# One product of the output stage computed by Strassen's method once more, with a sign flip, sums added by DMA, and work moved between VectorE, ScalarE and GpSimd

## The chip, the cores and the metric

The kernel runs on one core of a Trainium2 chip. The metric is the device time of one execution, in microseconds. The kernel before takes 2399.43 us, the median of three runs that lie between 2399.35 and 2399.5.

Five engines work beside each other and wait for each other through semaphores: TensorE (PE; its weight loads are shown apart as PEld), VectorE (DVE), ScalarE (ACT), GpSimd (POOL) and SyncE (SP, which here only starts DMAs). Each has one stream of instructions in a fixed order.

## The reference

The reference is a short causal convolution along the sequence, followed by a two-layer feed-forward block with a hard-swish gate. All is fp32.

```python
# x (8, 4096, 192), weight (8, 7), moe_w_in (192, 2048), moe_w_out (2048, 192)
w = softmax(weight, axis=-1)                       # per head, 7 taps
out = np.einsum('hk,bskhg->bshg', w, x_unf)        # x_unf: 7 shifted copies of x
h = out.reshape(B * S, D) @ w_in                   # 32768 tokens, 192 -> 2048
relu6 = np.clip(h + 3.0, 0.0, 6.0)
g = h * relu6 / 6.0
return (g @ w_out).astype(np.float32)              # 2048 -> 192
```

## The kernel before

**Tiling.** The 32768 tokens are cut into 32 blocks of 1024. A block has two groups of 512 tokens: group 0 lies on partitions 0 to 63 of the tile `x` and of its convolved form `y`, group 1 on partitions 64 to 127; a DMA (`swap`) copies the halves crosswise, so that each half of the partitions has its own group and the other one (`OWN`, `OTHER`). Block 0 has a path of its own. Blocks 1 to 31 go through two stages, one block after the other, and nearly all of the time is in them.

**The h stage** (`h_phase`, about 38 us a block) computes h = y @ w_in and the gate. It goes by 4 units of the hidden dimension, each with a lower (L) and an upper (U) stream of matmuls on the two halves of TensorE's rows. The order within a unit is written out by hand in `FIRST`, `SECOND` and `OTHERS`: `LP7` is "lower stream, product P7", `LAF` is the VectorE addition at L415 that makes one psum bank out of another one and a saved one, `R` is the relu on ScalarE (L329), `G` the gate on VectorE (L333). A prime means that the step belongs to the unit before, so the last gates of unit u are in the plan of unit u+1. `LP7` accumulates into the bank that `LAF` has just read, so it has to wait for `LAF`; it is the sixth product of the lower stream. `X` stands for what the block before left over (a transpose and its stores).

The result is `g`, in four blocks: `A11` and `A21` are the first half of the hidden dimension for groups 0 and 1, `A12` and `A22` the second half.

**The output stage** (`out_strassen`, about 36 us a block, for blocks 1 to 30; `out_last` for block 31) computes g @ w_out as a 2 by 2 block product in Strassen's form (Winograd's variant): seven products A11·B11, A12·B21, S4·B22, A22·T4, S1·T1, S2·T2, S3·T3, where the S are sums of blocks of g and the T sums of blocks of `w_out`. Each has 96 output rows, as three pieces of 32; TensorE runs four pieces side by side on four column groups. `a11_round` is one round of such matmuls: it computes two of the three pieces of A11·B11 by Strassen's method once more (matmuls 256 tokens wide at L545) and fills the round with the third piece, a piece of A12·B21 and a half of another. Then come `three(4, 2, 1)` (A22·T4), `rest_of_2` (L598), and three rounds for S3, S2 and S4, each with a third of S1·T1 as its fourth stream.

**Who makes the sums.** S3 (L517, 128x1024 for each unit) and the four sums for the inner Strassen of A11 (`a11_sums`, L537, 128x256) are on GpSimd, unit by unit in the h stage; those of the last unit run when the output stage has begun. S1 = A21 + A22 is added in place by DMA (L443). S2 and S4 are on VectorE (L517, two instructions of 128x2048 each).

**VectorE's order in the output stage** is that of the program: the last gates of the h stage; the seven taps of the next block's convolution (L271 and L275, 128x1536 each); seven small additions of the round just computed (L641, 32x256); S2; three additions and one more small one for A12·B21; S4; the output sums, transposes and stores, among them `y_sums` (L296) for the next block; and then `LAF` of the next block's h stage.

Of the kernel before, what the change touches and what calls it, by code (L numbers as in the profile page):

```python
# [16 lines left out]
def kernel(  # L17
# [7 lines left out]
):  # L25

# [24 lines left out]
    G = 2  # L51
# [102 lines left out]
    w_q = cst.tile([P, 4, UNITS, QS], F32, name="w_q")  # L154
# [64 lines left out]
    def w_sums():  # L219

        def sub(out, x, y):
            nc.gpsimd.tensor_tensor(out=out, in0=x, in1=y, op=ALU.subtract)

        for o, x, y in ((T1, B12, B11), (T3, B22, B12), (T2, B22, T1), (T4, T2, B21)):
            sub(w_out[:, :, o], w_out[:, :, x], w_out[:, :, y])
        y11, y12, y21, y22 = (
            w_out[:, c::2, B11, q * QS : (q + 1) * QS] for c in range(2) for q in range(2)
        )
        t1, t2, t3, t4 = (w_q[:, j] for j in range(4))
        for o, x, y in ((t1, y12, y11), (t3, y22, y12), (t2, y22, t1), (t4, y21, t2)):  # L230
            sub(o, x, y)
        b11, b12, b21, b22 = (w_in[:, c::2, s] for s in range(2) for c in range(2))
        t1, t2, t3, t4 = (w_in_t[:, j] for j in range(4))
        for o, x, y in ((t1, b12, b11), (t3, b22, b12), (t2, b22, t1), (t4, b21, t2)):
            sub(o, x, y)
# [24 lines left out]

    def conv_units(i, parts, cuts=1):


        x = x_tiles.pop(i)
        W = N // cuts

        def tap(part, k, t):
            c = c_sb[:, k : k + 1]
            to = y[:, part, t : t + W]
            if k == 0:  # L270
                nc.vector.tensor_scalar(  # L271
                    out=to, in0=x[:, part, t : t + W], scalar1=c, scalar2=None, op0=ALU.mult
                )
            else:
                nc.vector.scalar_tensor_tensor(  # L275
                    out=to, in0=x[:, part, k + t : k + t + W], scalar=c, in1=to,
                    op0=ALU.mult, op1=ALU.add,
                )

        return [  # L280
            lambda part=part, k=k, t=t: tap(part, k, t)
            for part in parts for k in range(KC) for t in range(0, N, W)
        ]
# [44 lines left out]
    def relu(r6, h):  # L328
        nc.scalar.activation(r6, h, ACT.Relu, bias=half[:], scale=1.0 / 6.0)  # L329
# [48 lines left out]
    class Unit:  # L378
# [7 lines left out]
        def run(self, op):  # L386
# [13 lines left out]
            if op in mms:  # L400
                to, w, third = mms[op]
                first = op in ("P1", "P5")
                if first:
                    bank[to] = take()
                half_mm(k, bank[to], w, third, first, True, not first)
            elif op == "F1":
                bank["b"] = take()
                nc.scalar.copy(out=psum[:, bank["b"]], in_=psum[:, bank["a"]])  # L408
            elif op == "CE":
                self.p5 = p5s.tile([P, N], F32, name="p5")  # L410
                nc.scalar.copy(out=self.p5[:], in_=psum[:, bank["e"]])  # L411
                give(bank["e"])
            elif op in ("AF", "AD"):
                to = bank[op[1].lower()] = take()
                nc.vector.tensor_tensor(  # L415
                    out=psum[:, to], in0=psum[:, bank["b"]], in1=self.p5[:], op=ALU.add
                )
            elif op[0] == "R":
                r6 = self.r6[op[1]] = rs.tile([P, N], F32, name="r6")
                relu(r6[:], psum[:, bank[op[1]]])  # L420
            else:
                group, c = self.results[op[1]]
                b = bank[op[1]]
                gate(g_of(2 * u + c, group, k), self.r6[op[1]][:], psum[:, b])
                give(b)

    def h_phase(left):
        work = {(u, k): Unit(u, k) for u in range(UNITS) for k in range(2)}
        for u, plan in enumerate(PLANS):
            for step in plan:  # L430
                if step == "X":
                    while left:
                        left.pop(0)()
                    continue
                op = step[1:].rstrip("'+")
                at = u + (step[-1] == "+") - (step[-1] == "'")
                if at < UNITS:
                    work[at, "LU".index(step[0])].run(op)
            if u:
                slots = slice(2 * u - 2, 2 * u)  # L440
                g_sums(nc.gpsimd, (3,), range(NP)[slots], 2)

                nc.gpsimd.dma_start(  # L443
                    out=S1[:, slots], in_=A22[:, slots], accum_op=ALU.add
                )
            if u < UNITS:
                a11_sums(u)
# [32 lines left out]
    def out_direct(i, work):  # L480

        parts = [(k, q) for k in range(G) for q in range(G * NQ)]
        for r in range(0, len(parts), 4):
# [17 lines left out]
            xt = ot.tile([P, N], F32, name="xt")  # L501
            nc.vector.transpose(out=xt[:], in_=bank)
# [4 lines left out]
    def g_sums(engine, which, slots, width):  # L507

        forms = {
            3: (S3, A11, A21, ALU.subtract),  # L510
            2: (S2, S1, A11, ALU.subtract), 4: (S4, A12, S2, ALU.subtract),
        }
        for n in which:
            o, a, b, op = forms[n]
            for p in slots[::width]:
                r = slice(p, p + width)
                engine.tensor_tensor(out=o[:, r], in0=a[:, r], in1=b[:, r], op=op)  # L517

# [9 lines left out]
    X11, X12, X21, X22 = (A11[:, c::2, t : t + TH] for t in (0, TH) for c in range(2))  # L528

    def a11_sums(u):  # L530

        s1, s2, s3, s4 = (sums[:, n, u] for n in range(4))
        for o, a, b, op in (
            (s1, X21[:, u], X22[:, u], ALU.add), (s3, X11[:, u], X21[:, u], ALU.subtract),
            (s2, s1, X11[:, u], ALU.subtract), (s4, X12[:, u], s2, ALU.subtract),
        ):
            nc.gpsimd.tensor_tensor(out=o, in0=a, in1=b, op=op)  # L537
# [15 lines left out]
    def a11_round(i, p1, p2):  # L553

        ba, bb = take(), take()
        a, b = (psum[:, n] for n in (ba, bb))
        y11, y12, y21, y22 = (
            w_out[:, k::2, B11, q * QS : (q + 1) * QS] for k in range(2) for q in range(2)
        )
        t1, t2, t3, t4 = (w_q[:, n] for n in range(4))  # L560
        s1, s2, s3, s4 = (sums[:, n] for n in range(4))
        m0 = (
            quarters(a, 0, first_half, X11, y11) + quarters(a, 0, second_half, X12, y21)
# [3 lines left out]
            quarters(a, 1, first_half, X22, t4)  # L567
            + quarters(a, 1, second_half, A12[:, ::2, first_half], w_out[:, ::2, B21, rows(2)])
            + quarters(b, 1, first_half, s1, t1) + quarters(b, 1, second_half, s4, y22)
        )  # L570
        m2, m3 = product(a, 2, 1, 2), product(a, 3, 2, 0)
        for n in range(NP):
            for mms, k in ((m0, 2 * n), (m1, 2 * n), (m2, n), (m3, n),
                           (m0, 2 * n + 1), (m1, 2 * n + 1)):
                mms[k]()
        mp = cs.tile([P, TH], F32, name="mp")
        r1, r2, r3 = (mp[rows(n)] for n in range(3))
        nc.scalar.copy(out=r1, in_=a[rows(0), first_half])
        piece(p1, 2, a, 2)
        piece(p2, 0, a, 3)  # L580
        add(p1[rows(0), first_half], r1, a[rows(0), second_half])
        add(r2, r1, b[rows(0), first_half])
        add(r3, r2, b[rows(0), second_half])
        add(p1[rows(0), second_half], r3, a[rows(1), first_half])
        add(p1[rows(1), second_half], r3, b[rows(1), first_half])
        add(r2, r2, b[rows(1), first_half])
        add(p1[rows(1), first_half], r2, b[rows(1), second_half])
# [3 lines left out]
    def rest_of_2(a):  # L591
# [3 lines left out]
        w = w_out[:, :, B21, rows(2)]  # L595
        for p, tokens in ((1, slice(0, N)), (0, second_half)):
            for j in range(4):
                nc.tensor.matmul(  # L598
                    out=bank[rows(j), tokens], lhsT=w[:, 2 * j + p],
                    rhs=A12[:, 2 * j + p, tokens], start=bool(p), stop=True,  # L600
                    tile_position=(0, j * QS), skip_group_check=True,
                )
# [40 lines left out]
    def store(i, c, k, half_, qs=range(NQ), queues=(nc.sync,), tokens=slice(0, N)):  # L643

        xt = ot.tile([P, N], F32, name="xt")
# [4 lines left out]

    def sums_tiles():
        return (cs.tile([DH, N], F32, name=f"c{k}") for k in range(6))
# [3 lines left out]
    def out_last(i):  # L656
# [19 lines left out]
        add(u2[:], p1[:], bank[m])  # L676
# [4 lines left out]
        add(p4[two], u3[two], p4[two], ALU.subtract)  # L681
# [7 lines left out]
        for t in range(0, N, N // 2):  # L689
# [9 lines left out]
            add(u3[rows(2), ts], u3[rows(2), ts], bank[rows(NQ), ts], ALU.subtract)  # L699
# [3 lines left out]
    def out_strassen(i, conv):  # L703
# [3 lines left out]
        ba, a = a11_round(i, p1, p2)  # L707
        g_sums(nc.vector, (2,), every, 4)
        b, bank = three(4, 2, 1)
        nc.scalar.copy(out=p4[:], in_=bank[m])  # L710
        piece(p2, 1, bank, NQ)
        give(b)
        swap(slice(0, K3))
        b, bank = rest_of_2(a)
        pieces(p2, 2, bank)
        give(b)
        add(p2[rows(2), first_half], p2[rows(2), first_half], a[rows(1), second_half])
        give(ba)
        g_sums(nc.vector, (4,), every, 4)
# [7 lines left out]
        add(u2[:], p1[:], bank[m])  # L727
# [3 lines left out]
        add(p4[:], u3[:], p4[:], ALU.subtract)  # L731
# [27 lines left out]
    with tc.manual_schedule():  # L759
# [115 lines left out]
        cs = ctx.enter_context(tc.tile_pool(name="cs", bufs=1))  # L875
        ot = ctx.enter_context(tc.tile_pool(name="ot", bufs=4))
# [8 lines left out]
        sums = ss.tile([P, 4, UNITS, N // 2], F32, name="sums")  # L885
        left = []
        for i in range(1, NB):
            h_phase(left)
# [39 lines left out]
```

## Time and profile before

The page of the profile has a span of 2397.1 us.

| engine | busy us | share |
|---|---|---|
| PE | 2388.7 | 100% |
| DVE | 2138.0 | 89% |
| PEld | 1105.0 | 46% |
| ACT | 1087.9 | 45% |
| POOL | 836.4 | 35% |

One block (block 10) in stretches, from the profile's table of busy time by window. It starts with the h stage at 764.28 us and ends where the next h stage starts.

| stage | us | PE | DVE | ACT | POOL |
|---|---|---|---|---|---|
| h stage | 38.08 | 38.08 | 31.79 | 27.79 | 20.01 |
| `a11_round` | 6.90 | 6.90 | 6.80 | 1.26 | 5.61 |
| `three(4, 2, 1)` | 6.87 | 6.87 | 6.73 | 1.52 | 0.00 |
| `rest_of_2` | 1.29 | 1.29 | 1.29 | 1.00 | 0.00 |
| S3, S2, S4 rounds | 20.72 | 20.72 | 20.19 | 1.90 | 0.00 |
| sum | 73.86 | 73.86 | 66.79 | 33.47 | 25.62 |

A matmul counts as busy from its start to its modelled end, and the next has started by then, so PE reads as busy throughout even where a start is late. DVE is busy nearly all of the output stage and has its idle time in the h stage.

### The profile page before, as it was taken

The page shows a single profiled execution, that of the slowest core. Times are in us where ns is not written, and L with a number is a line of the kernel's source. Part 1 is how long each engine was busy: PE and PEld are TensorE (multiplying, and loading weights), DVE is VectorE, ACT ScalarE, POOL GpSimd, SP SyncE. Part 2 cuts the span into 40 slices and gives each one's busy share as a digit, 9 for nine tenths or more (in the row PEclk, how much of TensorE's full clock was granted, in tenths as well). Part 3 has the DMA queues.
Part 4 walks back from the last instruction along what each step waited for, and adds up shares of the span by engine and source line. Part 5 has one row for each costly group of instructions (what it writes and reads, how often), then busy time and mean ns, then how long its engine had stood idle before and what let it go on. Part 6 is the DMA issues. An engine that isn't in the chain of part 4 may idle for free.

```text
span 2397.1 us, 43036 instructions
## 1 busy us (share of the span) xinstructions
PE 2388.7 (100%) x17496; PEld 1105.0 (46%) x17496; DVE 2138.0 (89%) x2773; ACT 1087.9 (45%) x1858; POOL 836.4 (35%) x780
## 2 busy tenths in 40 slices
PE   9999999999999999999999999999999999999998
PEld 6444444444444444444454444444444444444443
DVE  8798889988899988899888998889998889988896
ACT  7234553345543355433454334553445543455433
POOL 2524432234422344223443224432234422344222
PEclk9999999999999999999999999999999999999999
DMA  5233333323333233333333333333323233333322
GB/s 146 46 56 64 62 61 64 67 50 69 59 59 66 53 73 60 60 58 57 67 63 58 67 57 59 63 67 58 67 52 73 54 65 59 55 70 63 58 51 43
DMA packets 261143, 149.86 MB, mean 63 GB/s; under 512 B 207504, under 2 KB 212624, under 8 KB 260944
## 3 DMA queue, kind: packets, MB, share of 16 engines
q1 hardware_dynamic: 225880, 81.56, 16.9%
q0 software_dynamic: 33824, 65.28, 15.8%
q8 instruction: 137, 2.24, 0.4%
q14 instruction: 62, 0.51, 0.1%
q10 hardware_dynamic: 1240, 0.27, 0.1%
HBM read 31.72 MB, written 25.17 MB: 24 GB/s over the span
## 4 chain that ended last, share of the span: by engine, by line
PE 99%; DMA 0%; DVE 0%; SPq 0%; ACT 0%; issue 0%; DVEq 0%; ACTq 0%
PE psum L323 51%; PE psum L456 41%; PE psum L545 5%; PE psum L598 2%; DMA x<-in_x_dram 0%; DMA out_dram<-xt 0%; DVE c L641 0%; DVE xt L647 0%; SPq L106 0%; SPq L140 0%; DVE top L184 0%; PE psum L774 0%; DVE y L275 0%; SPq L95 0%; ACT y L788 0%
## 5 line engine op out<-in xcount | busy, mean ns | idle before, releaser
L456 PE MATMUL psum<-g,w_out 128*32 128x512 f32 (+1 forms) x7936 | 1120.0, 589 | 0.0
L323 PE MATMUL psum<-y,w_in 64*128 64x512 f32 x3664 | 884.8, 591 | 0.4 <-DVE y L275 0.3
L329 ACT ACTIVATE r<-psum,half 128x512 f32<-128x512 f32 x1024 | 641.0, 688 | 241.6 <-PE psum L323 234.8
L333 DVE SCALAR_TENSOR_TENSOR g<-r,psum 128x512 f32<-128x512 f32 x1024 | 641.7, 681 | 4.7 <-ACT r L329 1.5
L323 PEld LDWEIGHTS psum<-y,w_in 64*128 64x128 f32 x3664 | 441.6, 187 | 362.6 <-issue 292.2
L537 POOL TENSOR_TENSOR sums<-g 128x256 f32<-128x256 f32 x248 | 188.1, 831 | 1181.3 <-DVE g L333 1163.2
L456 PEld LDWEIGHTS psum<-g,w_out 128*32 128x32 f32 x7936 | 339.4, 110 | 460.3 <-issue 438.1
L323 PE MATMUL psum<-y,w_in_t 64*128 64x512 f32 x1984 | 524.5, 593 | 0.0
L415 DVE TENSOR_TENSOR psum<-psum,p 128x512 f32<-128x512 f32 x496 | 324.5, 694 | 193.1 <-PE psum L323 184.7
L633 ACT COPY c<-psum 32x512 f32<-32x512 f32 x218 | 126.0, 578 | 588.2 <-PE psum L456 571.0
L517 POOL TENSOR_TENSOR s<-g 128x1024 f32<-128x1024 f32 x124 | 293.8, 2369 | 245.5 <-PE psum L323 237.7
L275 DVE SCALAR_TENSOR_TENSOR y<-x,c_sb,y 128x1536 f32<-128x1536 f32 (+1 forms) x206 | 366.5, 1786 | 6.6
L323 PEld LDWEIGHTS psum<-y,w_in_t 64*128 64x128 f32 x1984 | 247.7, 186 | 195.2 <-issue 124.9
L517 DVE TENSOR_TENSOR g<-g 128x2048 f32<-128x2048 f32 x124 | 279.5, 2296 | 7.4 <-DMA g<-g 3.9
L456 PE MATMUL psum<-s,w_out 128*32 128x512 f32 x1488 | 218.9, 592 | 0.0
L408 ACT COPY psum<-psum 128x512 f32<-128x512 f32 x248 | 138.8, 571 | 71.7 <-PE psum L323 56.1
L443 POOL DMA_DIRECT2D g<-g x124 | 149.1, 1202 | 39.8 <-POOL s L517 39.8
L641 DVE TENSOR_TENSOR c<-c,psum 32x512 f32<-32x512 f32 (+2 forms) x219 | 139.8, 638 | 16.0 <-ACT c L633 9.7
L411 ACT COPY p<-psum 128x512 f32<-128x512 f32 x248 | 133.2, 591 | 41.1 <-PE psum L323 40.3
L456 PEld LDWEIGHTS psum<-s,w_out 128*32 128x32 f32 x1488 | 70.8, 110 | 129.2 <-issue 124.8
L545 PE MATMUL psum<-g,w_out 128*32 128x256 f32 x720 | 109.4, 380 | 0.0
L545 PE MATMUL psum<-sums,w_q 128*32 128x256 f32 x720 | 108.5, 379 | 0.0
(64 smaller groups left out, 1080.1 us busy)
## 6 DMA issues: line engine op xcount, KB each, us to landing
g<-g POOLq DMA_DIRECT2D x124, 512.0 KB, 5.0
out_dram<-xt SPq DMA_DIRECT2D x380, 64.0 KB, 2.0
y<-y SPq DMA_DIRECT2D x62, 384.0 KB, 4.7
x<-in_x_dram SPq DMA_DIRECT2D x55, 388.5 KB, 6.0
stage<-in_moe_w_in_dram SPq DMA_DIRECT2D x16, 192.0 KB, 4.4
stage<-in_moe_w_out_dram SPq DMA_DIRECT2D x8, 384.0 KB, 5.1
x<-in_x_dram SPq DMA_DIRECT2D x7, 384.0 KB
y<-y SPq DMA_DIRECT2D x6, 128.0 KB, 2.4
```

The costliest lines, as they stand in the source:

```text
L275: nc.vector.scalar_tensor_tensor(out=to, in0=x[:, part, k + t : k + t + W], scalar=c, in1=to, op0=ALU.mult, op1=ALU.add,)
L323: nc.tensor.matmul(out=psum[:, b], lhsT=w[r], rhs=y[r, third_of_y], start=start, stop=stop, skip_group_check=onto,)
L329: nc.scalar.activation(r6, h, ACT.Relu, bias=half[:], scale=1.0 / 6.0)
L333: nc.vector.scalar_tensor_tensor(out=out, in0=r6, scalar=1.0, in1=h, op0=ALU.min, op1=ALU.mult)
L408: nc.scalar.copy(out=psum[:, bank["b"]], in_=psum[:, bank["a"]])
L415: nc.vector.tensor_tensor(out=psum[:, to], in0=psum[:, bank["b"]], in1=self.p5[:], op=ALU.add)
L443: nc.gpsimd.dma_start(out=S1[:, slots], in_=A22[:, slots], accum_op=ALU.add)
L456: lambda p=p: nc.tensor.matmul(out=bank[j * QS : (j + 1) * QS, tokens], lhsT=w_out[:, p, w, cols], rhs=x[:, p, tokens], start=(first and p ...
L517: engine.tensor_tensor(out=o[:, r], in0=a[:, r], in1=b[:, r], op=op)
L537: nc.gpsimd.tensor_tensor(out=o, in0=a, in1=b, op=op)
L545: lambda u=u: nc.tensor.matmul(out=dst[rows(j), tokens], lhsT=w[:, u], rhs=x[:, u], start=(u == 0 and tokens == first_half), stop=(u == UN ...
L641: nc.vector.tensor_tensor(out=out, in0=x, in1=y, op=op)
```

## The change

The change does the following for blocks 1 to 30.

- A22·T4 gets the same treatment as A11·B11: `round_twice(1, ...)` replaces `three(4, 2, 1)`. Its inner sums (`quarter_sums(engine, 1, u)`, four of 128x256 for each unit) are added; `rest_of_2` shrinks, since the second round takes another half piece of A12·B21 with it. TensorE has fewer matmuls for it.
- Group 1 is negated: the taps use `c_sg`, whose upper half is minus the coefficients, the relu is given scale -1/6 for group 1, and so A21 and A22 come out with a minus sign. S2 is now a plain sum, S1 + A11, and a DMA with accumulation can make it: three quarters of it (slots 2 to 7) are added by three DMAs from GpSimd's queue, one quarter stays on VectorE.
- The first tap of the convolution goes from VectorE to ScalarE.
- The sums of the last unit (S3 of it, and the inner sums of A22) go to VectorE; the other units' stay on GpSimd.
- Work tiles of the output stage and the transposed tiles share memory with the inner sums.

```diff
-            if k == 0:
+            if k == 0 and i:
+                nc.scalar.mul(to, x[:, part, t : t + W], c)
...
+            last = u == UNITS
             if u:
+                engine = nc.vector if last else nc.gpsimd
                 slots = slice(2 * u - 2, 2 * u)
-                g_sums(nc.gpsimd, (3,), range(NP)[slots], 2)
+                if twice and not last:
+                    quarter_sums(engine, 1, u - 1)
+                g_sums(engine, (3,), range(NP)[slots], 2)
                 nc.gpsimd.dma_start(
                     out=S1[:, slots], in_=A22[:, slots], accum_op=ALU.add
                 )
-            if u < UNITS:
-                a11_sums(u)
+                if twice and last:
+                    quarter_sums(engine, 1, u - 1)
+            if not last and twice:
+                quarter_sums(nc.gpsimd, 0, u)
...
-        ba, a = a11_round(i, p1, p2)
-        g_sums(nc.vector, (2,), every, 4)
-        b, bank = three(4, 2, 1)
-        nc.scalar.copy(out=p4[:], in_=bank[m])
-        piece(p2, 1, bank, NQ)
-        give(b)
+        ba, a = round_twice(0, first_half, p1, (1, 2, p1), (2, 0, p2))
+        for c in range(2, NP, 2):
+            slots = slice(c, c + 2)
+            nc.gpsimd.dma_start(out=S2[:, slots], in_=S1[:, slots], accum_op=ALU.add)
+        g_sums(nc.vector, (2,), range(2), 2)
+        bb, b = round_twice(1, second_half, p4, (4, 2, p4), (2, 1, p2))
         swap(slice(0, K3))
-        b, bank = rest_of_2(a)
+        b2, bank = rest_of_2()
+        g_sums(nc.vector, (4,), every, 4)
         pieces(p2, 2, bank)
-        give(b)
-        add(p2[rows(2), first_half], p2[rows(2), first_half], a[rows(1), second_half])
+        give(b2)
+        for bank, tokens in ((a, first_half), (b, second_half)):
+            add(p2[rows(2), tokens], p2[rows(2), tokens], bank[rows(1), second_half])
         give(ba)
-        g_sums(nc.vector, (4,), every, 4)
+        give(bb)
```

Beside these, `w_sums` makes the four inner sums of T4 once at the start (GpSimd), and some subtractions become additions and the other way round.

## The prediction

> **What bounds the kernel now.** I read the table of busy time by window first (the table above). Every stage is full of PE, so the bound seems to be TensorE, and a block is 73.86 us. But DVE is at 6.80 of 6.90, 6.73 of 6.87 and 20.19 of 20.72 us in the output stage, so I asked next which engine is ahead of which where the output stage hands over to the next h stage. The list of waits has this, among longer ones of engines that have time:
>
> ```profile
> DVE psum L415 <- PE psum L323: 184.7, 120, 2.2
> PEld psum L323 <- DVE psum L415: 1.9, 7, 0.3
> ```
>
> The first line is the time that DVE has left inside the h stage: it waits for matmuls 120 times. The second says that in 7 places it is the other way round: a weight load waits for L415. That is `LP7` behind `LAF`. The timeline of block 11 at this place (start, length, engine; `LAF` is the first of two L415):
>
> ```profile
> 841.66 1.27 DVE L415 TENSOR_TENSOR psum<-psum,p 128x512 f32<-128x512 f32 x2
> ...
> 842.38 0.18 PEld L323 LDWEIGHTS psum<-y,w_in_t 64*128 64x128 f32 x1
> 842.55 0.19 PEld L323 LDWEIGHTS psum<-y,w_in 64*128 64x128 f32 x1
> ```
>
> `LAF` ends at 842.33 (841.659 + 0.671 in the trace), the load follows 0.05 us later, and its matmul starts at 842.546, still on the beat of 0.429 us. Counted from the start of this h stage (838.143), `LAF` ends at 4.19 and the matmul is due at 4.40; it can start 0.05 after `LAF`. So DVE has **0.16 us of slack per block**, no more. The trace also shows what happens beyond it. In the block whose h stage starts at 690.244, `LAF` ends at 4.52, the matmul starts at 4.57 instead of 4.40, and the period from that start to the next is 74.03 us instead of 73.87. The same happens in three more blocks. A late `LAF` goes into the time one for one.
>
> Why is it late there? The first taps of these two blocks, DVE and POOL:
>
> ```profile
> 804.38 1.80 DVE L271 TENSOR_SCALAR y<-x,c_sb 128x1536 f32<-128x1536 f32 x1
> ...
> 804.44 2.40 POOL L517 TENSOR_TENSOR s<-g 128x1024 f32<-128x1024 f32 x1
> ```
>
> ```profile
> 656.48 1.80 DVE L271 TENSOR_SCALAR y<-x,c_sb 128x1536 f32<-128x1536 f32 x1
> 658.32 2.60 DVE L275 SCALAR_TENSOR_TENSOR y<-x,c_sb,y 128x1536 f32<-128x1536 f32 x1
> ...
> 656.92 2.38 POOL L517 TENSOR_TENSOR s<-g 128x1024 f32<-128x1024 f32 x1
> ```
>
> The first tap has one tensor input and takes 1.80 beside POOL's S3. The second has two and takes 1.82 alone, 2.24 where POOL's S3 lies over 0.62 us of it (usual block), 2.60 where it lies over 0.97 us. DVE all but stops while POOL runs, and POOL hardly slows (2.36 to 2.40).
>
> **What the Trainium skill says.** *GPSIMD Engine Reference*, Specifications: GpSimd shares its SBUF interfaces with VectorE, and instructions of VectorE with two SBUF inputs contend. The taps agree, as just shown. *TensorE: Matmul & The Clock Gate*, Architectural detail: TensorE can pull weight loads ahead of running matmuls, ScalarE and VectorE are strict queues; its Step-by-step section adds that matmuls stay in program order. The late `LAF` agrees: nothing overtakes `LP7`. *VectorE: DVE Perf Modes*, The TRN2 errata, prices an fp32 tensor_tensor of N elements at (N + 151)/0.96 ns. The trace has 2296 ns for 2048 (price 2291) and 675 to 700 for 512 (price 691), so I use the price, called an estimate, for widths that DVE doesn't run from SBUF now: 1.22 us for 1024, 0.42 for 256.
>
> **The change on TensorE.** In units of one 512-wide product of a 32-row piece, the output stage has 144 + 4 wide ones and 32 + 4 half-wide ones, 148 + 18 = 166; after it has 128 + 4 and 64 half-wide ones, 132 + 32 = 164. A unit costs 6.90/32 = 0.216 us in the mixed round and 6.87/32 = 0.215 in a wide one, so half-wide matmuls cost just half. Two units fewer are **0.43 us a block**, over 30 blocks 12.9 us. Without any wait that is the whole gain.
>
> **The change on VectorE**, from the last gate of the h stage to `LAF`, where DVE has no gap (804.38 to 841.66, 37.28 us). Removed: the first tap, 1.84 with its gap; S2, two of 2048, 4.53 (from 820.72 to 825.25); the 0.42 us by which POOL stretches the second tap, since the taps now start some 3 us later, when POOL is through. Together 6.79. Added: S3 of the last unit, 1.22; the four inner sums of A22, 4 x 0.425 = 1.70; the quarter of S2, 1.22; the seven small additions of the second round, 3.07 as the first round's (817.65 to 820.72); one more addition of 256, 0.44. Together 7.65. **Net +0.86 us.** Both ends for the unseen widths: 0.36 each for the inner sums, if independent ones overlap as the gates do, gives 0.60 in all; the price is the upper end and I take it.
>
> **What POOL adds to it.** Per unit POOL now has inner sums of A11 (3.0 us, from 782.57 to 785.56), the same for A22 (3.0), S3 (2.36 and 0.30 before the DMA), DMA issue until the next starts (1.10): 9.75 to 9.86 us, and a unit of the h stage is 9.45 (781.44 to 790.90). It falls 0.3 to 0.4 us behind in each of three units. The last inner sums of A11 end 2.12 us after the start of the output stage now (804.49), so at 3.0 to 3.35 then. DVE's S3, with two SBUF inputs, starts at 2.1 and is held up for 0.9 to 1.25 us; with the small discount the taps show (0.62 of overlap cost 0.42, 0.97 cost 0.78) that is 0.75 to 1.05. I take 0.90. VectorE's way becomes 0.86 + 0.90 = **1.76 us longer**.
>
> **The sum.** TensorE comes to `LP7` 0.43 us earlier, `LAF` 1.76 later, 0.16 is slack: `LP7` waits 0.43 + 1.76 - 0.16 = 2.03 us. A block costs 2.03 - 0.43 = 1.60 us more; 30 h stages follow such an output stage: +48.0 us. 2399.4 + 48.0 = **2447 us**.
>
> **Edits that I cost at nothing.** The first tap on ACT (some 1.6 us, from 388 ns for 128 and 723 ns for 512 elements at L786 and L788) runs after the last relu and is done before DVE gets through its sums; ACT then has nothing until the round ends. Queued behind POOL's DMA for the last S1 are the three S2 DMAs; they wait for matmuls that read A11, are issued by about 8 us after the start of the round, land in 5.0 each, and S4, the first to need them on DVE, comes at about 25. The S2 round of TensorE starts at 21.5, and the quarter of S2 on DVE is done at 21.7 by the sums above: at most some 0.2 us there, which would be taken out of the wait at `LP7`, not added. Inner sums on POOL, ready by 3.4, are needed at about 4.5. The bank of the S3 round, needed by the fifth product of the next h stage at 1.8 us, is free at about 1.7: close, but not beyond `LP7`. The four sums of T4 at the start (as those of B11, 6.4 us) end POOL at 96.7 instead of 90.3; the first product that needs POOL's weights is due at 100. Signs cost nothing.
>
> **Rivals.**
> 1. VectorE's way doesn't get longer than its slack, for instance because sums overlap and moves pay more than I think: time is 2399.4 - 12.9 = **2386.5**. For it speaks the count of elements: what DVE loses, 1536 + 4096, is more than what it gains for S3, inner sums and S2, 1024 + 1024 + 1024. Against it: the eight small additions that no count of elements shows, 3.5 us of fixed cost mostly. It would take a net of -0.27.
> 2. The same as my forecast, but no hold-up by POOL, because the last inner sums of A11 aren't late or S3 starts after them: net 0.86 - 0.16 = 0.70 a block, **2420**. With the low end of 0.60: 0.44, 2413.
> 3. POOL is later than worked out and DVE's S3 stands for all of 1.25 us or more: 0.86 + 1.25 - 0.16 = 1.95, **2458**; if the rounds also wait for POOL, beyond it.
>
> **How the numbers follow.** Forecast 0.60, rival 2 0.23, rival 3 0.07, rival 1 0.07; 0.03 for a net close to the slack, where gain and wait cancel. The range goes from 2414, near the low end of rival 2, to 2459, rival 3. Faster 0.07, same 0.03, slower 0.90.
>
> **What would show it.** In the profile after: weight loads of L323's successor waiting for the successor of L415 in all 30 blocks, near 2 us each (about 60 in total, 1.9 now); a period near 75.5; DVE's 128x1024 sum taking about 2.1 us, not 1.2, beside POOL's 128x256 ones; second taps all at 1.82; round windows of 6.9 and 6.9, and 0.86 for `rest_of_2`. It is wrong if no such wait is there or if the longest wait of PE is another one, such as S2 or a psum bank.

## The result, and the profile after

The changed kernel takes **2426.55 us**, the median of runs that lie between 2426.17 and 2426.84; the kernel before takes 2399.4. The ratio is 1.0113 (95% interval 1.0096 to 1.0131), so the change costs 27.1 us, 0.90 us for each of the 30 h stages that follow a changed output stage. The forecast was 2447: the direction and the place are right, and 1.60 us a block was too much.

In the changed kernel every line has a new number: the matmuls of the h stage are L338, `LAF` is one of the additions at L430, S3, S2 and S4 are L541, the inner sums L565, the taps L290 (the first one, on ScalarE, L284), the small additions L669, and the DMAs for S2 L750. The page's first part gives busy time, share and instructions by engine:

```profile
PE 2408.2 (99%) x18216; PEld 1249.3 (52%) x18216; DVE 2158.3 (89%) x3105; ACT 1143.4 (47%) x1919; POOL 1117.4 (46%) x1187
```

TensorE is busy 19.5 us longer, although it has two units of work less in each block: a matmul that stands in front of a wait is still counted as busy (the h stage in the windows below reads 39.07 us busy of 39.34, with a wait of 1.29 us in it). The busy shares hardly tell the two kernels apart. The chain of work that ended last does. Before and after:

```profile
PE 99%; DMA 0%; DVE 0%; SPq 0%; ACT 0%; issue 0%; DVEq 0%; ACTq 0%
```

```profile
PE 46%; DVE 45%; issue 7%; POOL 0%; DVEq 0%; DMA 0%; SPq 0%; ACT 0%; POOLq 0%; ACTq 0%
```

VectorE now carries nearly half of it. The list of waits names the place (us in total, times, longest):

```profile
DVE psum L430 <- PE psum L338: 180.5, 93, 2.2
...
PEld psum L338 <- DVE psum L430: 45.1, 70, 1.5
...
PE psum L338 <- DVE psum L430: 9.0, 28, 0.7
```

The second line was 1.9 us in 7 places. It is the wait of `LP7` for `LAF`. Its 70 times are not 70 blocks: several loads and matmuls of one place are counted, so the timeline has to say what one block loses. Block 11, around that place:

```profile
851.81 0.67 DVE L430 TENSOR_TENSOR psum<-psum,p 128x512 f32<-128x512 f32 x1
...
852.54 0.29 PEld L338 LDWEIGHTS psum<-y,w_in_t 64*128 64x128 f32 x2 [1.10 <-DVE psum L430]
```

The h stage starts at 846.86. `LAF` ends at 852.49, 5.63 us into it (4.19 before); the matmul starts 0.05 later, at 5.69 instead of 4.40. It waits **1.29 us**. In the other 29 blocks `LAF` ends 5.4 to 6.1 us into the h stage. The same block by windows (length, then busy us and count of PE, PEld, DVE, ACT, POOL, then clock, DMA share, GB/s), in the order h stage, first and second round, `rest_of_2`, the three other rounds:

```profile
846.86:886.20 39.34, 39.07 (x178) 21.71 (x176) 33.06 (x55) 27.73 (x47) 27.89 (x32) 1.00 0.35 63
886.20:893.10 6.90, 6.90 (x98) 3.89 (x100) 6.83 (x11) 2.75 (x4) 5.44 (x7) 1.00 0.65 110
893.10:900.00 6.90, 6.90 (x103) 4.14 (x98) 6.79 (x4) 1.52 (x3) 1.88 (x2) 1.00 1.11 186
900.00:900.86 0.86, 0.86 (x16) 0.37 (x10) 0.82 (x2) 0.00 (x0) 0.00 (x0) 1.00 1.10 191
900.86:921.60 20.74, 20.74 (x196) 8.60 (x188) 19.91 (x30) 3.25 (x6) 0.00 (x0) 1.00 0.35 69
sum 74.74, PE 74.47 PEld 38.72 DVE 67.42 ACT 35.25 POOL 35.21; mean PE 14.89 PEld 7.74 DVE 13.48 ACT 7.05 POOL 7.04
```

The output stage is shorter, 35.40 us against 35.78, and the h stage longer, 39.34 against 38.08: the gain of the matmuls is there (0.38 us), and three times as much is lost in the stage whose matmuls the change does not touch. The difference of the periods is about 0.88 in this block.

What VectorE does after the last gate on the way to this `LAF` (S4, the output sums and the stores follow):

```profile
813.48 1.54 DVE L541 TENSOR_TENSOR s<-g 128x1024 f32<-128x1024 f32 x1
814.94 0.75 DVE L565 TENSOR_TENSOR sums<-g 128x256 f32<-128x256 f32 x2
815.61 0.41 DVE L565 TENSOR_TENSOR sums<-sums,g 128x256 f32<-128x256 f32 x1
816.06 0.43 DVE L565 TENSOR_TENSOR sums<-g,sums 128x256 f32<-128x256 f32 x1
816.40 11.08 DVE L290 SCALAR_TENSOR_TENSOR y<-x,c_sg,y 128x1536 f32<-128x1536 f32 x6
827.40 3.11 DVE L669 TENSOR_TENSOR sums<-sums,psum 32x256 f32<-32x256 f32 x7
830.54 1.23 DVE L541 TENSOR_TENSOR g<-g 128x1024 f32<-128x1024 f32 x1
```

From 813.48 to the start of `LAF` at 851.81 there are 38.33 us, against 37.28 before. VectorE's way is **1.05 us longer**. With 0.16 of slack that is 0.89 a block, times 30 it is 26.7, close to the 27.1 that were measured.

GpSimd at the same time:

```profile
810.61 1.81 POOL L565 TENSOR_TENSOR sums<-g 128x256 f32<-128x256 f32 x2
811.98 1.13 POOL L565 TENSOR_TENSOR sums<-sums,g 128x256 f32<-128x256 f32 x1
813.19 0.75 POOL L565 TENSOR_TENSOR sums<-g,sums 128x256 f32<-128x256 f32 x1
```

Its last inner sum ends at 813.94, and VectorE's S3 starts at 813.48: they lie over one another for 0.46 us, where the prediction had 0.9 to 1.25.

### The profile page after: what moved, and what is told of

Its sections match the earlier page's. It is cut to its first block, busy times and chain, and to the rows that moved or that the text cites. A ratio compares the mean times of both kernels' runs of the same rounds, so it can differ in the third digit from the quotient of the medians.

```text
span 2425.0 us, 45845 instructions
## 1 busy us (share of the span) xinstructions
PE 2408.2 (99%) x18216; PEld 1249.3 (52%) x18216; DVE 2158.3 (89%) x3105; ACT 1143.4 (47%) x1919; POOL 1117.4 (46%) x1187
## 4 chain that ended last, share of the span: by engine, by line
PE 46%; DVE 45%; issue 7%; POOL 0%; DVEq 0%; DMA 0%; SPq 0%; ACT 0%; POOLq 0%; ACTq 0%
PE psum L338 40%; DVE sums L669 15%; DVE y L290 11%; DVE g L541 7%; PE psum L480 5%; DVE g L348 5%; DVE y L311 3%; DVE s L541 2%; DVE psum L430 2%; DVE sums L565 1%; DVE sums L675 1%; PE psum L573 1%; DMA x<-in_x_dram 0%; POOL sums L565 0%; POOL s L541 0%
## 5 line engine op out<-in xcount | busy, mean ns | idle before, releaser
L338 PE MATMUL psum<-y,w_in 64*128 64x512 f32 x3664 | 889.6, 591 | 0.2 <-DVE y L290 0.2
L565 POOL TENSOR_TENSOR sums<-g 128x256 f32<-128x256 f32 x420 | 323.9, 857 | 1013.7 <-DVE g L348 962.4
L338 PEld LDWEIGHTS psum<-y,w_in 64*128 64x128 f32 x3664 | 472.1, 187 | 333.1 <-issue 272.1
L338 PE MATMUL psum<-y,w_in_t 64*128 64x512 f32 x1984 | 528.2, 597 | 9.2 <-DVE psum L430 9.0
L430 DVE TENSOR_TENSOR psum<-psum,p 128x512 f32<-128x512 f32 x496 | 323.7, 694 | 188.4 <-PE psum L338 180.5
L661 ACT COPY sums<-psum 32x512 f32<-32x512 f32 x248 | 143.5, 579 | 479.6 <-PE psum L480 476.2
L338 PEld LDWEIGHTS psum<-y,w_in_t 64*128 64x128 f32 x1984 | 252.0, 186 | 225.4 <-issue 123.7
L669 DVE TENSOR_TENSOR sums<-sums,psum 32x256 f32<-32x256 f32 (+1 forms) x669 | 322.7, 486 | 31.9 <-ACT sums L661 10.7
L290 DVE SCALAR_TENSOR_TENSOR y<-x,c_sg,y 128x1536 f32<-128x1536 f32 x186 | 342.6, 1842 | 7.1 <-ACT y L284 1.6
L541 POOL TENSOR_TENSOR s<-g 128x1024 f32<-128x1024 f32 x93 | 219.5, 2361 | 51.9 <-PE psum L338 51.5
L573 PE MATMUL psum<-g,w_out 128*32 128x256 f32 x1440 | 218.1, 380 | 0.0
L573 PE MATMUL psum<-sums,w_q 128*32 128x256 f32 x1440 | 217.0, 379 | 0.0
L541 DVE TENSOR_TENSOR g<-g 128x2048 f32<-128x2048 f32 (+1 forms) x94 | 180.7, 1949 | 5.8 <-DMA g<-g 2.6
L465 POOL DMA_DIRECT2D g<-g x124 | 149.1, 1202 | 68.3 <-DVE s L541 34.8
L565 POOL TENSOR_TENSOR sums<-sums,g 128x256 f32<-128x256 f32 x210 | 179.1, 853 | 0.0
```

The source lines that it names most:

```text
L290: nc.vector.scalar_tensor_tensor(out=to, in0=x[:, part, k + t : k + t + W], scalar=c, in1=to, op0=ALU.mult, op1=ALU.add,)
L338: nc.tensor.matmul(out=psum[:, b], lhsT=w[r], rhs=y[r, third_of_y], start=start, stop=stop, skip_group_check=onto,)
L430: nc.vector.tensor_tensor(out=psum[:, to], in0=psum[:, bank["b"]], in1=self.p5[:], op=ALU.add)
L465: nc.gpsimd.dma_start(out=S1[:, slots], in_=A22[:, slots], accum_op=ALU.add)
L565: engine.tensor_tensor(out=o, in0=a, in1=b, op=op)
L573: lambda u=u: nc.tensor.matmul(out=dst[rows(j), tokens], lhsT=w[:, u], rhs=x[:, u], start=(u == 0 and tokens == first_half), stop=(u == UN ...
```

## The experiments

The experiments ask three things: whether the late `LAF` alone makes the time and at one for one; what each part of the change is worth; and what GpSimd does to VectorE. In the ratios, each kernel is set against the kernel before on the same chip, which took 2399.1 to 2399.3 us.

### One and three more small additions in the kernel before

This tests the rule of the prediction, "0.16 us of slack, then one for one", with nothing else of the change.

```diff
         add(p1[rows(0), first_half], r1, a[rows(0), second_half])
+        add(p1[rows(0), first_half], r1, a[rows(0), second_half])
         add(r2, r1, b[rows(0), first_half])
```

> The kernel before with one of its small additions of the output stage (32x256) done twice, 0.44 us of VectorE a block and nothing else. Theory (0.16 us of slack at LAF, then one for one): 0.28 us a block in 30 blocks, 2399.4 + 8.4 = 2407.8 us. Rival (VectorE is only 89% busy and has several us of slack a block): no change, 2399.4.

The time was 2407.29 us (1.0033, 1.0021 to 1.0046), 8.0 more. VectorE's way is 0.43 us longer in the trace (37.67 against 37.24 in one block), for which the rule gives 30 x (0.43 - 0.16) = 8.1. The second kernel has the same line four times, three more than before.

> The kernel before with one small addition of the output stage done four times, 1.33 us more of VectorE a block. Theory: 1.33 - 0.16 = 1.17 us a block, 2399.4 + 35 = 2434.5 us. Rival (several us of slack a block): no change, 2399.4.

It took 2433.51 us (1.0143, 1.0129 to 1.0157), 34.3 more. VectorE's way is 1.32 us longer in the trace (38.56 us), and the rule gives 30 x (1.32 - 0.16) = 34.8. With TensorE's work untouched, 17% of the chain now goes through VectorE:

```profile
PE 80%; DVE 17%; issue 1%; DMA 0%; ACT 0%; SPq 0%; DVEq 0%; ACTq 0%
```

TensorE does not lose all of it at `LP7`. `LAF` ends at 5.11 and makes `LP7` 0.76 us late; the other 0.38 is lost in the output stage (36.17 us instead of 35.79), whose rounds for S2 and S4 now wait for VectorE's sums:

```profile
PEld psum L456 <- DVE g L517: 54.0, 60, 1.2
...
PEld psum L323 <- DVE psum L415: 27.1, 65, 0.6
```

The prediction had said of S2 that such a wait is taken out of the one at `LP7` and not added to it, and so it is. What counts one for one is the length of VectorE's way, at whichever of its results TensorE waits.

VectorE was 89% busy, and yet 1.3 us more of its work in 74 cost 1.14: idle time in the h stage does not help a chain of work that has none between the last gate and `LAF`.

### All of S2 by DMA

If the wait is `LAF`'s lateness, taking the last quarter of S2 (1.23 us) from VectorE takes it away.

```diff
-        for c in range(2, NP, 2):
+        for c in range(0, NP, 2):
             slots = slice(c, c + 2)
             nc.gpsimd.dma_start(out=S2[:, slots], in_=S1[:, slots], accum_op=ALU.add)
-        g_sums(nc.vector, (2,), range(2), 2)
```

> The changed kernel with all four quarters of S2 added by DMA and none by VectorE. Theory (VectorE's way to LAF sets the block): VectorE's way is 1.26 us shorter, a block 74.77 - 1.26 = 73.51 us, close to TensorE's own 73.43: about 2389 us, faster than the kernel before. Rival (TensorE's half-wide matmuls or DMA traffic cost the time): no gain, 2426 or more, as there is one more DMA of 512 KB a block.

The time was **2390.84 us** (0.9966, 0.9953 to 0.9979), faster than the kernel before. The wait of `LP7` in its list:

```profile
PEld psum L338 <- DVE psum L430: 11.7, 43, 0.4
```

`LAF` now ends at 4.36 to 4.59 us into the h stage in most blocks, at 4.94 in the latest, and the chain is PE for 99% again. So the whole loss of the change lay in 1.2 us of VectorE's work a block. The half-wide matmuls and the DMAs, which the rival blames, are all still there.

### All of S2 and one quarter of S4 by DMA

The kernel of the last experiment still had `LAF` up to 0.2 us late in most blocks. One quarter of S4 more goes to DMA.

```diff
-        g_sums(nc.vector, (4,), every, 4)
+        nc.gpsimd.dma_start(out=S4[:, 6:8], in_=S2[:, 6:8], accum_op=ALU.add)
+        g_sums(nc.vector, (4,), range(4), 4)
+        g_sums(nc.vector, (4,), range(4, 6), 2)
```

> All of S2 by DMA as before, and the last quarter of S4 (slots 6 and 7) by one more DMA; the rest of S4 stays on VectorE. Theory: VectorE's way is 1.1 us shorter than with S2 alone (one of 128x1024 instead of one of 128x2048), so that LAF is early in every block and only TensorE's own 73.43 us are left: about 2387 us. The DMA lands some 28 us after the start of the output stage and is needed at 33.5. Rival (DMA is the limit from here on, as when all of S4 went by DMA): TensorE waits for the DMA in its last round, 2391 or more.

It took **2386.56 us** (0.9948, 0.9936 to 0.9961), the best of all kernels here. In the list of waits:

```profile
PEld psum L338 <- DVE psum L430: 2.4, 12, 0.3
```

That is as little as before the change. `LAF` ends at 4.09, and a block takes 73.47 us against 73.87, 0.40 less where the prediction had 0.43 for two units less on TensorE. So two half-wide matmuls cost nearly what one wide one costs. That the time agrees with the prediction's 2399.4 - 12.9 = 2386.5 to a tenth is in part luck: the blocks account for about 12 us of it, the rest lies outside them.

### All of S2 and all of S4 by DMA

> The changed kernel with all of S2 and all of S4 added by DMA; VectorE makes neither. S4's four DMAs wait for the matmuls that read A12 (14.7 us after the start of the output stage), are issued one after the other by about 20 us and land by about 25, before the S4 round at 28.4. Theory: VectorE's way is 5.7 us shorter and no longer sets anything; the block is TensorE's own 73.43 us, 12.9 us in all below the kernel before: 2386.5 us, and hardly better than with S2 alone. Rival (TensorE's half-wide matmuls cost more than half of a wide one, or DMA traffic costs the time): 2426 or more. If S4 lands late, TensorE waits in its last round instead, and the trace names the DMA.

```diff
-        g_sums(nc.vector, (4,), every, 4)
+        for c in range(0, NP, 2):
+            slots = slice(c, c + 2)
+            nc.gpsimd.dma_start(out=S4[:, slots], in_=S2[:, slots], accum_op=ALU.add)
```

This stands on top of S2 by DMA. It took 2531.38 us (1.0543, 1.0522 to 1.0565). The way out that the expectation left open is what came: matmuls of the output stage now wait for these transfers.

```profile
PEld psum L480 <- DMA g<-g: 217.7, 120, 3.5
...
PE psum L480 <- DMA g<-g: 111.5, 101, 2.6
```

The DMA view of one such output stage (tiles, queue, times, KB each, median us from issue to landing):

```profile
g<-g POOLq DMA_DIRECT2D x9, 512.0 KB, 12.1
y<-y SPq DMA_DIRECT2D x2, 384.0 KB, 10.8
```

In the kernel before these took 5.0 and 4.7 us. With twelve accumulating transfers a block instead of four, the stage moves some 190 GB/s without a break, and each transfer lands behind those before it. What was free for S2 and a quarter of S4 is not free for the rest.

### The first tap back on VectorE

```diff
-            if k == 0 and i:
-                nc.scalar.mul(to, x[:, part, t : t + W], c)
-            elif k == 0:
+            if k == 0:
                 nc.vector.tensor_scalar(
```

> The changed kernel with the first tap on VectorE again, as before the change. Theory (VectorE's way to LAF sets the block): 1.84 us more in each of 30 blocks, one for one: 2426.5 + 55 = 2482 us. Rival (TensorE's half-wide matmuls with their additional weight loads, or the additional DMA traffic, cost the time): VectorE has room, the time stays within 5 us of 2426.

It took 2482.99 us (1.035, 1.0334 to 1.0365), 56.4 more than the changed kernel or 1.88 a block: the tap's 1.84, one for one, to 0.04. Of this TensorE loses 1.15 us in the h stage (40.52 us against 39.37 in the typical block of the changed kernel) and 0.70 in the output stage (36.10 against 35.40), where its S2 round waits for VectorE's quarter of S2:

```profile
PEld psum L478 <- DVE g L539: 43.6, 30, 1.8
```

So the move to ScalarE was worth all of VectorE's time for it. The changed kernel's list of waits has `DVE y L290 <- ACT y L284` only once, for 1.6 us, so VectorE does not wait for ScalarE's tap.

### The last unit's sums on GpSimd

The prediction charged the sums on VectorE with 2.92 us of work and 0.90 of hold-up. This kernel gives them back.

```diff
-                engine = nc.vector if last else nc.gpsimd
+                engine = nc.gpsimd
```

> The changed kernel, but the sums of the last unit (S3 and the four inner sums of A22) are made by GpSimd again, not by VectorE. Theory (VectorE's way to LAF sets the block, and GpSimd's sums hold up VectorE's two-input instructions): VectorE gives up 2.92 us of own work a block, but its second tap can start only when ScalarE's first tap is done (some 0.8 us of waiting), and then GpSimd's S3 and inner sums, 2.36 + 2.9 us, lie beside the taps and hold them up for 4.2 us or so. Net some 2.1 us a block more: about 2489 us. Rival (only VectorE's own instructions count, GpSimd beside it is free): 2.92 - 0.8 = 2.1 us less a block, more than is lost; the block falls to TensorE's 73.43 us and the time to about 2387 us.

It took 2540.36 us (1.0586, 1.0568 to 1.0603), 113.8 more than the changed kernel: slower, as the theory had it, but by nearly twice the 62 us that it gave. VectorE's taps:

```profile
1084.20 14.37 DVE L290 SCALAR_TENSOR_TENSOR y<-x,c_sg,y 128x1536 f32<-128x1536 f32 x6 [0.76 <-ACT y L284]
...
1111.34 2.29 DVE L541 TENSOR_TENSOR g<-g 128x2048 f32<-128x2048 f32 x1 [3.01 <-DMA g<-g]
```

and GpSimd beside them:

```profile
1087.26 3.41 POOL L565 TENSOR_TENSOR sums<-g 128x256 f32<-128x256 f32 x2
1090.64 2.25 POOL L565 TENSOR_TENSOR sums<-sums,g 128x256 f32<-128x256 f32 x1
1092.97 2.13 POOL L565 TENSOR_TENSOR sums<-g,sums 128x256 f32<-128x256 f32 x1
1095.05 3.66 POOL L750 DMA_DIRECT2D g<-g  x3
```

The six taps take 14.37 us instead of 11.08, the first tap from ScalarE is waited for (0.76), and 2.92 of sums are gone: 3.29 + 0.76 - 2.92 = 1.13 us more, about half of what the theory gave, since the hold-up is 3.29 and not 4.2. The rest comes from the order of GpSimd's queue, which the theory did not think of: the DMAs for S2 stand behind the inner sums and are issued only at 1095.05. S4 on VectorE waits for them, 3.01 us here and 2.4 in the mean of the 30 blocks, and so does TensorE in its S2 round:

```profile
PE psum L480 <- DMA g<-g: 59.7, 28, 2.6
```

TensorE's stages show the same two parts: the h stage is 1.1 us longer than in the changed kernel (40.47 against 39.37) and the output stage some 2.7 (about 38.1 against 35.40), together the 3.8 a block that were measured. How much of the 2.7 is VectorE's wait and how much TensorE's own is not separated.

### GpSimd sums of unrelated data beside the taps

The last experiment mixes the hold-up with a later DMA. Here GpSimd's work depends on nothing and nothing depends on it: to the kernel with all of S2 by DMA, two additions of constant tiles are added behind the DMAs for S2. Their result is not used.

```diff
+        for _ in range(2):
+            nc.gpsimd.tensor_tensor(
+                out=scratch[:], in0=w_in_t[:, 0], in1=w_in_t[:, 1], op=ALU.add
+            )
```

> All of S2 by DMA, and GpSimd adds two constant tiles into a scratch tile twice a block (two of 128x512, two inputs each, 1.28 us each alone), in the stretch in which VectorE runs the taps; nothing reads the result. Theory (GpSimd holds up VectorE's two-input instructions): the taps take some 2.1 to 2.6 us longer and the block with them, about 2390.8 + 66 = 2457 us. Rival (GpSimd's work is free for VectorE): 2391 us, as VectorE has not one instruction more.

It took 2461.53 us (1.026, 1.0246 to 1.0274), 70.7 more than without these additions, 2.36 a block. The groups of instructions of this kernel (times, busy us, mean ns of one, idle before):

```profile
L290 DVE SCALAR_TENSOR_TENSOR y<-x,c_sg,y 128x1536 f32<-128x1536 f32 x186 | 415.5, 2234 | 7.1 <-ACT y L284 1.6
...
L752 POOL TENSOR_TENSOR scratch<-w_in_t 128x512 f32<-128x512 f32 x60 | 134.0, 2234 | 2.4
```

A tap takes 2234 ns in the mean, 1842 in the kernel without these additions: 6 x 0.392 = 2.35 us a block, all that the kernel lost. GpSimd working beside VectorE, with no data in common, stops VectorE for 73 us (415.5 less 186 x 1.842) while it works for 134.

## Why the prediction was right, and where its size was off

**The bound** was right. `LP7` waits for `LAF`, the slack is 0.16 us, and beyond it time goes one for one: the two kernels with more small additions show it at 8.0 and 34.2 us, the changed kernel at 27.1 for 1.05 us. The shares of busy time, with VectorE at 89%, show nothing of it. What the prediction said of `LP7` alone holds for VectorE's way as a whole: with more of it, the S2 and S4 rounds wait too.

**TensorE** was right: 6.90, 6.90 and 0.86 in the windows as forecast, and 0.38 to 0.40 us a block won where 0.43 was forecast.

**VectorE's work.** The taps at 1.82 each (11.08 for six), the seven small additions at 3.11 and the quarter of S2 at 1.23 came close to their prices. For the last the price was an estimate from the formula in *VectorE: DVE Perf Modes*, The TRN2 errata, 1.22. The price for the inner sums was for one at a time. Each does take 412 to 467 ns, but the first two overlap, and the four take 1.46 us from first start to the taps (814.94 to 816.40) and not 1.70. The prediction had seen this lower end (0.36 each, 1.44) and taken the upper.

**GpSimd's hold-up** is the term that was mis-sized: 0.90 us forecast, about 0.3 measured. The group of S3 on VectorE, in the same columns as above, beside one of the same size and kind that has no GpSimd beside it:

```profile
L541 DVE TENSOR_TENSOR s<-g 128x1024 f32<-128x1024 f32 x31 | 46.2, 1490 | 0.0
L541 DVE TENSOR_TENSOR g<-g 128x1024 f32<-128x1024 f32 x30 | 36.8, 1226 | 0.9
```

Forecast was about 2.1 us for it; it takes 1.49, so the hold-up is 0.26 us. The loss for a given overlap was right: the prediction's own two cases, 0.42 for 0.62 and 0.78 for 0.97, are the overlap less 0.2, and here 0.46 us over one another cost 0.31, the overlap less 0.15. The overlap was wrong, because GpSimd is less late than forecast. The prediction let it fall 0.3 to 0.4 us behind in each of three units. GpSimd's issues of the DMA for S1, which end a unit's work, before and after:

```profile
781.44 1.20 POOL L443 DMA_DIRECT2D g<-g  x1 [0.30 <-POOL s L517]
...
790.90 1.20 POOL L443 DMA_DIRECT2D g<-g  x1 [0.30 <-POOL s L517]
```

```profile
865.32 1.20 POOL L465 DMA_DIRECT2D g<-g  x1 [0.30 <-POOL s L541]
...
874.93 1.20 POOL L465 DMA_DIRECT2D g<-g  x1 [0.30 <-POOL s L541]
...
884.55 1.20 POOL L465 DMA_DIRECT2D g<-g  x1 [0.30 <-POOL s L541]
```

They are 9.61 and 9.62 us apart instead of 9.46, so GpSimd falls 0.16 behind in each of two units and not 0.3 to 0.4. The difference is the price of the inner sums of A22: it was taken from A11's, which stand behind a DMA issue and read 3.0, and A22's take 2.87 (866.43 to 869.40 to 872.27 are A11's and A22's in this trace). In the first of the three units it hardly falls behind: counted from the start of the output stage the first issue comes at -20.90 us, -20.92 before. Part of that is probably owed to the wait at `LP7` itself: in the kernel in which TensorE does not wait (a quarter of S4 by DMA) the first issue is at -20.75, and the last inner sum ends at 2.62. Here the last inner sum of A11 ends 2.5 us after the start of the output stage, with 2.12 before and 3.0 to 3.35 forecast.

*GPSIMD Engine Reference*, Specifications, says that instructions of VectorE with two SBUF inputs contend with GpSimd for the SBUF interfaces that they share, and the runs agree: the taps take 2234 ns instead of 1842 beside unrelated sums. It gives no size, and the sizes here are measured.

**The sum.** S3 and the inner sums take 2.92 us (813.48 to 816.40) where 3.82 were forecast: 0.66 from the hold-up's term, 0.24 from the inner sums. The other terms together came 0.19 longer than priced, which leaves 1.05 instead of 1.76. So the total came nearer than its terms: 0.90 too much in two of them and 0.19 too little in the others partly cancel, and that is luck. Put into the prediction's own formula, 0.43 + 1.05 - 0.16 gives a wait of 1.32 (1.29 measured), and less 0.43 it gives 0.89 a block (0.90 measured). Only the sizes went wrong, not the way in which they count.

**The rivals.** The first (2386.5) needed, by its own sum, a VectorE's way that is 0.27 us shorter; it was 1.05 longer. The second (2420, no hold-up) comes nearest: it left out the 0.3 that there is. The third (2458) asked for more lateness of GpSimd than forecast, 0.9 us and more; there is 0.4.

**Edits costed at nothing.** These held: no wait of TensorE for a psum bank, for S2 or for ScalarE's tap is new. The three DMAs for S2 took 7.3, 9.1 and 9.6 us to land before the `LAF` shown, where 5.0 were forecast. They run beside one another and the last of S1; that this makes them slower was not tested alone. Nothing waited for it. With all of S4 in the same queue it was no longer free.

## What to carry to other kernels

Where an engine at 100% hands over to one that is nearly full in one stage, look for the first matmul of the next stage that must wait, and measure how long before its due time the other engine is through; that slack, and not the busy share, is the room for more work, and beyond it each tenth of a microsecond counts in each block. A saving on the bounding engine is only cashed when the work that it creates elsewhere fits this slack: the same two matmul units cost 27 us or won 13, by where two quarters of sums, 2.3 us of VectorE's time, were made. When work is handed to another engine or to DMA, ask what it slows there while it runs, and what stands behind it in that queue.

## What the runs showed of the hardware

- VectorE and GpSimd, each with a two-input instruction, take turns here: the one that comes second stands until the first is through. A tap (1.82 us alone) that starts while GpSimd's addition runs takes longer by the overlap less 0.20 us: by 0.42 for 0.62 in the kernel before, by 1.77 for 1.98 beside S3 where the last unit's sums are on GpSimd, by 0.90 for 1.10 beside the unrelated sums. VectorE's S3 takes longer by the overlap less 0.14 in all the kernels where it runs (0.25 for 0.39 up to 0.58 for 0.73).
- It goes the other way too. GpSimd's 128x256 sums that start within a tap end 0.59 us after it (0.73 alone), its 128x512 additions 1.14 us after it (1.28 alone). GpSimd's S3, which the prediction read as hardly slowed (2.36 to 2.40), was there first. One case is open: the first unrelated addition starts, as shown, within a tap, and yet ends first (986.17 to 987.94), and the tap loses the time from its own start on (985.59 to 989.57). So there is little gain in running them side by side: 73 us lost on VectorE and 60 x 0.95 = 57 on GpSimd in 134 us.
- GpSimd's inner sums behind its own DMA issue are shown as longer (1.81 us for two and 1.13 for the third, against 0.75 for the fourth). But the four end 4.13 to 4.18 us after the start of the issue whether they are shown to start 0.8 or 1.1 us after it, which is the issue's 1.20 and the 2.9 that they take without one. So they run after the issue, not slower beside it, as far as the ends show.
- Accumulating DMAs of 512 KB within SBUF reach about 190 GB/s together. At four a block one lands after 5.0 us in the median. With twelve a block the nine of one output stage have a median of 12.1, and the 384 KB swap of y goes from 4.7 to 10.8 beside them.
